# Two sets of exponentials: exponents first, copies moved to VectorE, one piece moved behind the set

## The chip, the cores and the metric

The kernel runs on one core of a Trainium2 chip. A core has TensorE (PE, matrix products into PSUM), VectorE (DVE), ScalarE (ACT, functions looked up in a table that has to be loaded for each set of functions), GpSimd (POOL) and SyncE (SP), which here only issues DMAs. Each engine works through its own list of instructions in order and waits at semaphores for the others. The metric is the device time of one execution in microseconds; the figure for a kernel is the median of its runs.

## The reference

The reference computes one block of a network on an input of 2048 tokens by 448 channels: a modulation from a small vector, a layer norm, a long convolution by a state-space kernel (S4D), then a second layer norm and a token-mixing MLP with 1792 hidden units. What matters here is the convolution kernel:

```python
A = -jnp.exp(log_A_real) + 1j * A_imag
C = (C_real + 1j * C_imag) * dt[:, None]
P = jnp.exp((A * dt[:, None])[:, :, None] * pos[None, None, :])
K = 2.0 * jnp.einsum("dn,dnl->dl", C, P).real
y = jnp.fft.irfft(Uf * Kf[None, :, :], L2)[:, :, :L]
```

For each of 448 channels, 256 complex exponentials are evaluated at 2048 positions and summed to K; K is then convolved with the input by Fourier transforms of length 4096.

## The kernel before, in words

A position is split in two, l = 64 i + j, so that the sum over the 256 modes becomes a small matrix product of two factors, `E` (64 columns) and `G` (32 columns). The channels go by in 56 steps, each of 16 channels and one half of the modes; `st_kgen(s)` makes step s's part of K out of `E` and `G` on TensorE (64 small products into the PSUM tile `kg`, line 717).

The factors are magnitudes times sines and cosines. Magnitudes need ScalarE's table of exponentials and sines another table, so the kernel works in batches of eight steps: `window(s)`, called for s = 0, 8, ..., 48, makes the exponentials of the eight steps s to s + 7 in one go. For each e from 0 to 7 it issues two exponentials (`st_exp`, line 650, tile `mag`), then on TensorE the exponents of the next step (`st_exponents`, line 644, by the helper of line 627, tiles `xe` and `xg`), or behind the last of them the phases of step s (`st_phase`). The PSUM tiles `xe` and `xg` have two buffers each. GpSimd follows with two multiplications per step (`st_mag2`, lines 666 and 671). Behind the set come the eight steps themselves: `st_step` has six ScalarE functions (two absolute values, lines 683 and 684, written to `ab` and `gs`, and four sines, lines 685 to 688), four multiplications on VectorE (lines 692 to 696) and two on GpSimd (690 and 691).

Other work is laid in between. `st_s1` makes the first stage of K's Fourier transform for a pair of finished groups (product `y`, line 755) and copies it out of PSUM to `yk` (line 761). In the steps above 32 the convolution itself goes on in pieces, `piece(go, inside)`: a forward product (`pc_s2`, tile `kx`, line 809), a multiplication by the input's transform on VectorE (`pc_mul`, tiles `z`, line 817), an inverse product (`pc_inv`, tile `vv`, line 832) and a copy out of PSUM (`pc_out`, tile `vt`, line 842) that is stored by DMA. A piece that starts also loads what the piece three later needs (`pc_load`: `u`, line 781, and the table `si`, line 787). The tiles `y`, `kx` and `vv` share three PSUM buffers (`ms`); `kg` has one.

The order on TensorE, ScalarE, VectorE and GpSimd is the order in which the program issues the instructions (a manual schedule). SyncE's DMAs are ordered by a planner. Copies and multiplications that follow a product are not issued at once but kept in two lists, `act` and `dve`, and issued at the next `flush`: in the set once per e, in a step `dve` in the middle of `st_step` (`between`) and `act` behind it. So a copy on ScalarE of step s comes behind the six functions of step s + 1. `warm(n)` issues n products of constants without use, to keep TensorE busy; steps 8 k and 8 k + 1 have ten each.

Before the change, the inverse of piece 2 (then 7) stood in step 38 (46), the copies of that step's `y` were ScalarE's behind step 39 (47), the set had the `kg` product of step 39 (47) at e = 0, an inverse at e = 2, the start of a new piece at e = 4 and `y` at e = 5.

Of the kernel before, what the change touches and what calls it, by code (L numbers as in the profile page):

```python
# [29 lines left out]
NHALF = 2 * NG  # L30
BATCH = 8
# [201 lines left out]
def tile_adaln_s4d_mixer(ctx, tc, i, out):  # L233
# [19 lines left out]
    with ExitStack() as es:  # L253
# [124 lines left out]
        def flush(todo):  # L378
            while todo:
                todo.pop(0)()  # L380
# [260 lines left out]
        def st_exponents(s):  # L641
            g, h = divmod(s, 2)
            phs[s] = [pph.tile([P, 512], F32, tag=nm, name=nm) for nm in ("xe", "xg")]
            halves(phs[s], lex[g % 4][:, h * P : (h + 1) * P], tab[:, 2], True, True)

        def st_exp(s):
            mags[s] = mp.tile([P, 2, 512], F32, tag="mag", name="mag")
            pm = phs.pop(s)
            for k in range(2):
                S.activation(mags[s][:, k], pm[k], AF.Exp)  # L650

        def st_phase(s):

            g, h = divmod(s, 2)
            lhs = lph[g % 3][:, h * P : (h + 1) * P]
            pm = [pph.tile([P, 512], F32, tag=nm, name=nm) for nm in ("xe", "xg")]
            halves(pm, lhs, tab[:, 1], True, False)
            halves(pm, mg[:, 0], ones, False, False)
            halves(pm, mg[:, 1], ones, False, False)
            halves(pm, lhs, tab[:, 0], False, True)  # L660
            phs[s] = pm
# [37 lines left out]

        kgs, kss, made_k = {}, {}, [0]  # L700

        fresh, ready = [], []

        def mellow():
            ready.extend(fresh)
            fresh.clear()

        def st_kgen(s):
            g, h = divmod(s, 2)
            kg = kg_tile(g)  # L710
            made_k[0] += 1
            E, Gt = eg.pop(s)
            for m in range(4):
                for c in range(2):
                    for q in range(4):
                        d = 8 * (q // 2) + 2 * m + q % 2
                        T.matmul(  # L717
                            kg[32 * q : 32 * q + 32, m],
                            Gt[:, c, d],
                            E[:, c, d],  # L720
                            start=h == 0 and c == 0 and m == 0,
                            stop=h == 1 and c == 1,
                            skip_group_check=True,
                        )
            if h == 1:
                p, o = divmod(g, 2)
                if o == 0:
                    kss[p] = wp.tile([P, 2, 4, NJ], F32, tag="ks", name="ks")

                def copy():  # L730
                    S.copy(kss[p][:, o], kgs.pop(g)[:, 0:4])
                    if o:
                        dve.append(skip)

                def skip():
                    k0 = kss[p][:, :, :, 0:1]
                    G.tensor_tensor(k0, k0, dsk[:, g - 1 : g + 1, :, None], ALU.add)
                    fresh.append(p)

                act.append(copy)  # L740

        def st_s1(busy):

            if not ready:
                return False
            p = ready.pop(0)
            c, gl = divmod(p, NG // 4)
            ks = kss.pop(p)
            y1 = [pms.tile([P, 32, 2, 4, 2], F32, tag="ms", name="y1") for _ in range(2)]
            for o in range(2):  # L750
                for m in range(4):
                    for cc in range(2):
                        for q in range(2):
                            r = slice(64 * q, 64 * q + 64)
                            T.matmul(
                                y1[q][64 * cc : 64 * cc + 64, :, o, m], ks[r, o, m], wc[r, cc, r], start=True, stop=True
                            )

            def out(q, copy):
                o = yks[c][:, :, 2 * gl * GD : 2 * (gl + 1) * GD].rearrange("p k (g q m) -> p k g q m", g=2, q=2)  # L760
                copy(o[:, :, :, q], y1[q].rearrange("p k g m b -> p k g (m b)"))  # L761

            for q in range(2):
                (dve if busy else act).append(partial(out, q, V.tensor_copy if busy else S.copy))
            return True


# [223 lines left out]
                if k is not None:  # L991
                    f(k)

        def piece(go, inside=False):

            if pieces[1] < pieces[0]:
                n = pieces[1]
                pc_inv(n)
                (dve if inside else act).append(partial(pc_out, n, V.tensor_copy if inside else S.copy))
                pieces[1] += 1  # L1000
            if go:
                n = pieces[0]
                if n + 3 < 2 * NP:
                    pc_load(n + 3)
                pc_s2(n)
                dve.append(partial(pc_mul, n))
                pieces[0] += 1

        def window(s):
            if s:  # L1010
                aside.append(True)
            angle()
            logs(s == 8)
            if s == 8:
                u_scale()
                u_table(0)
                u_table(1)

            if s == 0:
                st_exponents(s)  # L1020
            for e in range(BATCH):
                st_exp(s + e)

                if e + 1 < BATCH:
                    st_exponents(s + e + 1)
                else:
                    st_phase(s)
                mellow()
                flush(dve)
                flush(act)  # L1030
                if s == 8 and e == 0:
                    tt(mod[1], mod[1], mod[2], ALU.mult)
                if s < 32:
                    more(WPACE[s // 8][e])
                if s == 0 and e >= 4:
                    u_stats(e - 4)
                if s == 8 and e in (3, 4):
                    modulation(0, e - 3)
                if s == 8 and e == 5:

                    G.tensor_tensor(mod[0], mod[0], mod[2], ALU.mult)
                if s and e < (2 if s <= 32 else 1):
                    st_kgen(s - (2 if s <= 32 else 1) + e)
                elif e == 5:
                    if s == 8:
                        yks[0] = y0.tile([P, 32, DC], F32, tag="yk", name="yk0")
                    st_s1(s > 16)

                for k, e0 in ((4, 1), (5, 3), (3, 6)) if s == 16 else ():
                    if e in (e0, e0 + 1):  # L1050
                        modulation(k, e - e0)

                if s == 8:
                    warm(7)
                if s in (8, 16):
                    some(u_rows, rows, (2, 2, 2, 2, 2, 0, 1, 1)[e])
                elif s == 24 and e in (0, 2, 4, 6, 7):
                    some(u_cols, cols, 1)

                if s >= 40 and e == 2:  # L1060
                    piece(False, True)
                if s >= 40 and e == 4:
                    piece(pieces[0] < NP, True)
                if s == 0 and e > 1:
                    st_mag2(e - 2)
                elif s and (e < 2 or s >= 32):
                    st_mag2(s + e)
                if s == 0 and e == 3:
                    for r in range(4):
                        dsk_copy(r)  # L1070
            aside.clear()
            if s == 0:

                S.activation(one, one, AF.Sin)
# [6 lines left out]
        for s in range(tail):  # L1081
# [11 lines left out]
            if s in late:  # L1093
                late[s]()
            if s < NHALF and s % BATCH == 0:
                window(s)
                if s == 0:
                    gp_ = right("gp", 3)
            if s % BATCH == 4:
# [12 lines left out]
            if s >= NHALF:  # L1112
                flush(dve)
                mellow()
            else:
                if s < 32 and s % BATCH > 1:
                    st_kgen(s - 2)
                if s % BATCH < 2:
                    warm(10)
                if (s + 1) % BATCH:  # L1120
                    st_phase(s + 1)
                elif s + 1 < NHALF:
                    st_exponents(s + 1)
                if s == 7:
                    warm(10)

                if s > 32 and s % BATCH:
                    st_kgen(s - 1)
                st_step(s, between)
# [4 lines left out]

            if s in (1, 2):
                x_load(4 + 4 * s, 4, G)
            free = s > 7 and not st_s1(s % BATCH == BATCH - 1)
            if s + 2 < 32 and (s + 2) % BATCH > 1 and s + 2 > 5:
                st_mag2(s + 2)

# [16 lines left out]
            if s == 31:  # L1157
                flush(dve)
                flush(act)
            if s > 32:  # L1160
                piece(pieces[0] < NP and (s % 2 == 1 or s >= NHALF))
            if s == 34:

                for t in (ft, b1, b2):
# [302 lines left out]
```

## Time and profile before

| | us |
|---|---|
| runs of the kernel before | 693.27, 698.49, 696.14 |
| median | 696.14 |
| span of the profiled execution | 693.5 |
| busy: PE, DVE, ACT, POOL | 628.4, 438.7, 446.6, 269.7 |
| set of step 40: table load, first exponential, first function of step 40 | at 260.14, 261.43, 270.92 |
| set of step 48: the same | at 302.19, 303.49, 313.93 |

The page gives no time of the profiled execution beside its span. Times in rows are microseconds from the start of the span; the second number of a row of instructions is how long it took. Rows in order of time merge neighbours of one kind (`x64`: 64 instructions). A bracket at the end says how long the engine stood idle before the instruction, and which instruction ended that. PEld is the loading of weights beside the products. The granted clock is the share of full clock at which TensorE was allowed to run.

### The profile page before, as it was taken

To read this page: it belongs to the slowest core of one execution; us is meant where nothing else is said; L and a number is where in the kernel's file an instruction comes from. 1 tells how busy PE (TensorE), PEld (TensorE's weight loads), DVE (VectorE), ACT (ScalarE), POOL (GpSimd) and SP (SyncE) were. 2 spreads that over 40 slices of the span, in tenths; PEclk is the share of its full clock that TensorE was granted. 3 is DMA by queue.
4 is the path that set the end of the run, shared out by engine and by line. 5 is a ranking of instruction groups with operands and counts; after the bars stand their busy time and mean duration, and the time that the engine had idled before them with its cause. 6 is when DMAs were issued, how large, how long until landed. Compare 5 with 4: busy or idle time off the path is not lost.

```text
span 693.5 us, 19319 instructions
## 1 busy us (share of the span) xinstructions
PE 628.4 (91%) x7706; PEld 452.3 (65%) x7706; DVE 438.7 (63%) x835; ACT 446.6 (64%) x847; POOL 269.7 (39%) x349
## 2 busy tenths in 40 slices
PE   0878999999888889988898899999999999999997
PEld 0444555444345545555554567778899999999997
DVE  7886789789785574856745578876732364444441
ACT  5888598999689889989856768887322352222220
POOL 7694669588499667767635300000000000000000
PEclk9989999999999899999899999999999999999999
DMA  7595557598786354443479899955574445556540
GB/s 174 176 208 130 196 186 247 200 225 258 219 253 189 94 131 140 131 125 104 116 251 341 280 269 261 262 151 142 177 226 108 146 132 160 160 162 170 163 131 26
DMA packets 100322, 125.16 MB, mean 180 GB/s; under 512 B 13860, under 2 KB 81992, under 8 KB 100232
## 3 DMA queue, kind: packets, MB, share of 16 engines
q1 hardware_dynamic: 99288, 121.30, 61.0%
q0 software_dynamic: 944, 2.62, 1.6%
q8 instruction: 61, 1.00, 0.6%
q14 instruction: 29, 0.24, 0.1%
HBM read 88.53 MB, written 34.87 MB: 178 GB/s over the span
## 4 chain that ended last, share of the span: by engine, by line
PE 62%; ACT 12%; POOL 8%; DMA 6%; DVE 5%; issue 5%; SPq 1%; DVEq 0%; POOLq 0%; ACTq 0%
PE o L1434 7%; PE acc L1270 6%; PE o L1433 6%; PE o L1435 6%; PE acc L1271 6%; PE acc L1272 6%; PE xe L627 5%; PE kg L717 4%; POOL G L691 3%; POOL G L690 2%; PE xg L627 2%; PE vv L832 2%; PE kx L809 2%; PE kg L639 2%; PE y L1307 2%
## 5 line engine op out<-in xcount | busy, mean ns | idle before, releaser
L218 ACT CAST whi<-w 128x896 fp32r<-128x896 f32 x64 | 59.7, 938 | 134.3 <-PE o L1434 82.6
L227 DVE TENSOR_TENSOR wlo<-w,whi 128x896 fp32r<-128x896 f32 x64 | 68.1, 1085 | 40.6 <-ACT whi L218 40.6
L690 POOL TENSOR_TENSOR G<-mag,gs 128x512 f32<-128x512 f32 x56 | 71.8, 1282 | 46.0 <-ACT gs L686 45.9
L1270 PE MATMUL acc<-h3h,whi 128*128 128x448 f32 x224 | 82.9, 370 | 1.7 <-ACT h3h L1337 0.9
L1271 PE MATMUL acc<-h3l,whi 128*128 128x448 f32 x224 | 81.6, 364 | 0.2 <-DVE mean L1291 0.2
L1434 PE MATMUL o<-ul,whi 128*128 128x448 f32 x224 | 81.3, 363 | 0.0
L1433 PE MATMUL o<-uh,whi 128*128 128x448 f32 x224 | 81.2, 362 | 0.0
L1272 PE MATMUL acc<-h3h,wlo 128*128 128x448 f32 x224 | 80.7, 360 | 0.0
L1435 PE MATMUL o<-uh,wlo 128*128 128x448 f32 x224 | 80.6, 360 | 0.0
L717 PEld LDWEIGHTS kg<-E,G 128*32 128x32 f32 x3584 | 58.1, 117 | 31.7 <-issue 22.1
L717 PE MATMUL kg<-E,G 128*32 128x64 f32 x3584 | 68.2, 231 | 4.1 <-issue 4.1
L691 POOL TENSOR_TENSOR G<-mag,gs 128x512 f32<-128x512 f32 x56 | 71.8, 1281 | 0.0
L627 PE MATMUL xg<-tab,lph 64*128 64x512 f32 x112 | 62.9, 561 | 8.0 <-DVE E L696 3.5
L627 PE MATMUL xe<-tab,lph 64*128 64x512 f32 x112 | 63.6, 568 | 1.9 <-ACT gs L687 0.9
L1438 DVE TENSOR_TENSOR y<-o,x 128x448 f32<-128x448 f32 x16 | 10.0, 624 | 78.8 <-PE o L1435 78.8
L692 DVE TENSOR_TENSOR E<-m,xe 128x512 f32<-128x512 f32 x53 | 36.3, 684 | 35.2 <-ACT xe L685 25.1
L671 POOL TENSOR_TENSOR m<-mag,w 128x512 f32<-128x512 f32 x53 | 55.8, 1052 | 4.1
L1270 PEld LDWEIGHTS acc<-h3h,whi 128*128 128x128 f32 x224 | 42.0, 188 | 15.2 <-ACT h L1342 3.5
L817 DVE TENSOR_TENSOR z<-kx,u 128x448 f32<-128x448 f32 x48 | 28.4, 619 | 33.1 <-PE kx L809 30.5
L832 PE MATMUL vv<-z,si 64*64 64x224 f32 x512 | 36.8, 385 | 9.4 <-ACT yk L761 6.2
L627 PE MATMUL xe<-tab,lex 64*128 64x512 f32 x56 | 31.0, 569 | 15.7 <-POOL wm L874 14.8
L1433 PEld LDWEIGHTS o<-uh,whi 128*128 128x128 f32 x224 | 42.1, 188 | 3.4
(242 smaller groups left out, 1455.9 us busy)
## 6 DMA issues: line engine op xcount, KB each, us to landing
w<-in_B_w_dram SPq DMA_DIRECT2D x64, 224.0 KB
w<-in_B_w_dram SPq DMA_DIRECT2D x32, 448.0 KB
yu_d<-yt SPq DMA_DIRECT2D x16, 448.0 KB
yi<-yu_d SPq DMA_DIRECT2D x32, 224.0 KB
us_d<-uo SPq DMA_DIRECT2D x16, 448.0 KB
u<-us_d SPq DMA_DIRECT2D x64, 112.0 KB
v_d<-vt SPq DMA_DIRECT2D x32, 224.0 KB
vt<-v_d SPq DMA_DIRECT2D x14, 448.0 KB
```

Of the source, the lines that this page charges most:

```text
L218: self.nc.scalar.copy(hi, w)
L227: eng.tensor_tensor(lo, w, hi.bitcast(F32), ALU.subtract)
L627: T.matmul(out[k], lhs[r], rhs[r], start=start, stop=stop)
L690: G.tensor_tensor(Gt[:, 1], mg_, v32(sg), ALU.mult)
L691: G.tensor_tensor(Gt[:, 0], mg_, v32(cg_), ALU.mult)
L717: T.matmul(kg[32 * q : 32 * q + 32, m], Gt[:, c, d], E[:, c, d], start=h == 0 and c == 0 and m == 0, stop=h == 1 and c == 1, skip_group_ch ...
L1270: nc.tensor.matmul(acc[f], hi[:, fs], h3h[:, r], start=r == 0, stop=False)
L1271: nc.tensor.matmul(acc[f], hi[:, fs], h3l[:, r], start=False, stop=False)
L1272: nc.tensor.matmul(acc[f], lo[:, fs], h3h[:, r], start=False, stop=r == 15)
L1433: nc.tensor.matmul(o, hi[:, ks], uh[kh][:, k], start=kh == 0 and k == 0, stop=False)
L1434: nc.tensor.matmul(o, hi[:, ks], ul[kh][:, k], start=False, stop=False)
L1435: nc.tensor.matmul(o, lo[:, ks], uh[kh][:, k], start=False, stop=kh == 1 and k == 6)
```

## The change

It concerns the sets of steps 40 and 48 alone (the new function `late_window`, called in place of `window` for s > 32) and the steps around them:

- The copies of `y` of step 38 (46) go into a list `hold` and are issued on VectorE at the start of the set. In that step no piece is called: the inverse that stood there waits. Step 39 (47) starts its piece as before but runs no inverse (`back=False`).
- In the set the `kg` product of step 39 (47) stands at e = 1 behind the exponents, with its copy on VectorE; the two inverses that are left over stand at e = 3 and e = 5, `y` at e = 6. All copies there are VectorE's.
- No new piece starts in the set. It starts in step 40 (48) instead, with its loads; its inverse comes in step 41 (49), which also starts the next piece.
- The ten products of `warm` are left out in steps 40 and 48.

```diff
-        def st_kgen(s):
+        def st_kgen(s, to=act):
...
-                    S.copy(kss[p][:, o], kgs.pop(g)[:, 0:4])
+                    (V.tensor_copy if to is dve else S.copy)(kss[p][:, o], kgs.pop(g)[:, 0:4])
...
-                act.append(copy)
+                to.append(copy)
...
-        def st_s1(busy):
+        def st_s1(*to):
...
-                (dve if busy else act).append(partial(out, q, V.tensor_copy if busy else S.copy))
+                to[-q].append(partial(out, q, S.copy if to[-q] is act else V.tensor_copy))
...
-        def piece(go, inside=False):
+        def piece(go, inside=False, back=True):
 
-            if pieces[1] < pieces[0]:
+            if back and pieces[1] < pieces[0]:
...
+        def late_window(s):
+
+            flush(hold)
+            for e in range(BATCH):
+                st_exp(s + e)
+                if e + 1 < BATCH:
+                    st_exponents(s + e + 1)
+                else:
+                    st_phase(s)
+                mellow()
+                flush(dve)
+                flush(act)
+                if e == 1:
+                    st_kgen(s - 1, dve)
+                elif e in (3, 5):
+                    piece(False, True)
+                elif e == 6:
+                    st_s1(dve)
+                st_mag2(s + e)
...
-                if s >= 40 and e == 2:
-                    piece(False, True)
-                if s >= 40 and e == 4:
-                    piece(pieces[0] < NP, True)
...
-                window(s)
+                (late_window if s > 32 else window)(s)
...
-                if s % BATCH < 2:
+                if s % BATCH < 2 and s != 40 and s != 48:
                     warm(10)
...
-            free = s > 7 and not st_s1(s % BATCH == BATCH - 1)
+            held = s > 32 and s % BATCH == BATCH - 2 and s + 2 < NHALF
+            free = s > 7 and not st_s1(hold if held else dve if s % BATCH == BATCH - 1 else act)
...
-            if s > 32:
-                piece(pieces[0] < NP and (s % 2 == 1 or s >= NHALF))
+            if s > 32 and not held:
+                ends = s % BATCH == BATCH - 1 and s + 1 < NHALF
+                piece(pieces[0] < NP and (s % 2 == 1 or s >= NHALF or s in (40, 48)), back=not ends)
```

More of the change, by code (lines that the diff above doesn't have):

```diff
@@ L700, in tile_adaln_s4d_mixer @@
         kgs, kss, made_k = {}, {}, [0]
-        fresh, ready = [], []
+        fresh, ready, hold = [], [], []
         def mellow():
@@ L1046, in window @@
                         yks[0] = y0.tile([P, 32, DC], F32, tag="yk", name="yk0")
-                    st_s1(s > 16)
+                    st_s1(dve if s > 16 else act)
                 for k, e0 in ((4, 1), (5, 3), (3, 6)) if s == 16 else ():
```

## The prediction

> **What bounds the kernel now.** I read the page first, then the chain of waits from 245 to 450 us, then the instructions in order of time around the sets of exponentials of steps 40 and 48 and the steps behind them, then TensorE's busy time with its granted clock by short stretches.
>
> ```profile
> PE 62%; ACT 12%; POOL 8%; DMA 6%; DVE 5%; issue 5%; SPq 1%; DVEq 0%; POOLq 0%; ACTq 0%
> ```
>
> ```profile
> 256.53 0.62 ACT xg L688
> 257.16 0.52 ACT yk L761
> 257.72 1.76 PE vv L832 x14
> ```
>
> The chain runs through PE for 62% of the span, but most of that is the MLP at the end. At the two sets it changes hands: ScalarE's sines of step 39, its copies of `yk`, then PE's piece, and from there PE's own products to the end of the set. The order of instructions at the entries to the sets of 40 and 48 says why:
>
> ```profile
> 257.05 1.10 ACT L761 COPY yk<-y 128x512 f32<-128x512 f32 x2
> 259.53 0.59 ACT L842 COPY vt<-vv 128x224 f32<-128x224 f32 x2 [1.38 <-PE vv L832]
> 260.14 1.28 ACT L650 ACT_TABLE_LOAD   x1
> 261.43 0.60 ACT L650 ACTIVATE mag<-xe 128x512 f32<-128x512 f32 x1
> ...
> 270.92 0.60 ACT L683 ACTIVATE ab<-xe 128x512 f32<-128x512 f32 x1
> ```
>
> ```profile
> 299.37 0.62 ACT L688 ACTIVATE xg<-ab 128x512 f32<-128x512 f32 x1
> ...
> 303.49 0.60 ACT L650 ACTIVATE mag<-xe 128x512 f32<-128x512 f32 x1
> 303.98 0.59 ACT L650 ACTIVATE mag<-xg 128x512 f32<-128x512 f32 x1
> ...
> 313.93 0.60 ACT L683 ACTIVATE ab<-xe 128x512 f32<-128x512 f32 x1
> ```
>
> The last sine ends at 256.53 + 0.62 = 257.15. Two copies of `yk` follow; the inverse products of a piece wait for their PSUM; ScalarE then idles 1.38 for that piece and copies it; only then come the table load and the first exponential. The sets run from first exponential to first `ab` in 270.92 - 261.43 = 9.49 and 313.93 - 303.49 = 10.44. Sixteen exponentials at a pitch of 303.98 - 303.49 = 0.49 are 7.8, so inside the sets TensorE is what ends last:
>
> ```profile
> 262.41 0.50 PE L627 MATMUL xe<-tab,lex 64*128 64x512 f32 x1
> 262.84 1.10 PE L717 MATMUL kg<-E,G 128*32 128x64 f32 x64
> ...
> 264.53 0.99 PE L832 MATMUL vv<-z,si 64*64 64x224 f32 x16
> ...
> 268.27 1.16 PE L755 MATMUL y<-wc,ks 64*64 64x64 f32 x64
> ...
> 270.19 0.58 PE L627 MATMUL xe<-tab,lph 64*128 64x512 f32 x1
> ```
>
> A block starts 0.07 before the one ahead of it ends (262.84 against 262.41 + 0.50), so from start to next start I count exponents 0.43, `kg` 1.03, a piece's inverse 0.92, `y` 1.09.
>
> **Entry.** The change takes the `yk` copies and the piece's copy off ScalarE here, and the inverse off PE. ScalarE then loads its table right behind the last sine, and 260.14 to 261.43 puts the first exponential 1.29 later: 257.15 + 1.29 = 258.44 instead of 261.43, and 299.37 + 0.62 + 1.29 = 301.28 instead of 303.49. That is 3.0 and 2.2 us earlier. The exponents it needs stand on PE behind the `y` of step 38, with no copy ahead of them now (by the chain it was `yk` that the piece between them waited for), so they are there before the last sine ends.
>
> **Inside the set.** PE's list has as many blocks as before: a second inverse comes in, the forward product (`kx`) goes out. Counted from the first exponential: its two reads end at 0.49 + 0.59 = 1.08, so the exponents for the third one end at about 1.65 and `kg` starts at 1.6. Then `kg` 1.03, two exponents 0.9, inverse 0.92, exponents 0.43 lead to 4.9; the next exponents wait for the buffer of the fifth exponential until 5.3; exponents 0.43, inverse 0.92, exponents 0.5 lead to 7.1; `y` waits 0.1 for VectorE's copy of the second inverse and takes 1.09, to 8.3. The phase product takes 1.2 by a later row (279.85 to the start of `kg` at 281.07, quoted below), and `ab` follows its end by 0.15 (270.19 + 0.58 to 270.92): 9.7. Against 9.49 and 10.44 that is 0.2 longer and 0.7 shorter. The sets together: -3.0 + 0.2 - 2.2 - 0.7 = -5.7. Bounds: no shorter than 13 x 0.49 + 0.59 + 1.2 + 0.15 = 8.3, when the phase product follows the seventh exponential at once (-8.5 in all), no longer than the 10.44 seen (-4.3).
>
> **What else is added there, and what hides it.** VectorE gets the held `yk` copies, the copy of `kg`, and one more piece:
>
> ```profile
> 262.53 1.16 DVE L817 TENSOR_TENSOR z<-kx,u 128x448 f32<-128x448 f32 x2 [4.06 <-PE kx L809]
> 265.57 0.69 DVE L842 COPY vt<-vv 128x224 f32<-128x224 f32 x2 [1.89 <-PE vv L832]
> ...
> 269.49 1.29 DVE L761 COPY yk<-y 128x512 f32<-128x512 f32 x2 [0.36 <-PE y L755]
> ```
>
> The `yk` pair is 1.29, the piece 0.69. A `kg` copy on VectorE does not occur in this trace: between 0.35 (half the 0.69) and 0.65 (half the 1.29), I take 0.38, nearest to ScalarE's 0.37 for it. That is 1.29 + 0.69 + 0.38 = 2.4 us into idle stretches of 4.06 and 1.89; without that cover `y` would start later by as much. Behind the held copies queues the multiplication `z`, whose reader, the inverse, now comes 3 us later. GpSimd's work in the set is unchanged and hangs on the exponentials alone: it is done 1.38 before its first `G` is wanted, in a set of 9.49, and in one of 9.7 that idle time doesn't shrink.
>
> ```profile
> 274.48 1.28 POOL L690 TENSOR_TENSOR G<-mag,gs 128x512 f32<-128x512 f32 x1 [1.38 <-ACT gs L686]
> ```
>
> The moved piece's loads move with it; the `u` load of piece 7 waits until piece 4 is multiplied, now in step 41, and holds SP's queue with a store of `v_d` and the next `lph` and `lex` loads behind it. Piece 7 is multiplied in step 46 and the loads behind serve steps 46 and later, so I cost this at nothing; without that cover the price would be one `u` load on the path.
>
> **The step behind.** Piece 4 now starts in step 40, is multiplied in step 41, and its inverse and piece 5's forward product both stand at the end of step 41.
>
> ```profile
> 277.72 0.68 DVE L693 SCALAR_TENSOR_TENSOR E<-mag,xe 128x512 f32<-128x512 f32 x1
> ...
> 281.83 1.15 DVE L817 TENSOR_TENSOR z<-kx,u 128x448 f32<-128x448 f32 x2
> ```
>
> ```profile
> 277.91 1.10 PE L717 MATMUL kg<-E,G 128*32 128x64 f32 x64
> 278.94 0.98 PE L809 MATMUL kx<-yk,si 128*64 128x224 f32 x8
> 279.85 0.50 PE L627 MATMUL xe<-tab,lph 64*128 64x512 f32 x1
> 281.07 1.10 PE L717 MATMUL kg<-E,G 128*32 128x64 f32 x64
> 282.60 1.05 PE L832 MATMUL vv<-z,si 64*64 64x224 f32 x16 [0.42 <-DVE z L817]
> ```
>
> ```profile
> 282.24 0.37 ACT L731 COPY ks<-kg 128x256 f32<-128x256 f32 x1 [0.19 <-PE kg L717]
> ```
>
> In these rows' times: `z` of piece 4 comes behind L693, 278.40 + 1.15 = 279.5; an inverse ends 0.67 after its `z` (283.65 against 282.98), 280.2; then `kx` 0.91, 281.1; the phase product 1.22, 282.3; `kg` 1.10, 283.4. ScalarE's copy of that `kg` then starts at 283.45 instead of 282.24, and behind it stand all sines of step 43: 1.2 us lost per set. The piece's own copy only moves from step 41's end to step 42's. Bounds 0 (ScalarE catches up from its small idle times) and 2.0 (the idle of step 34 below). Twice 1.2 gives +2.4.
>
> **The ten warming products taken out of steps 40 and 48.**
>
> ```profile
> 273.94 1.27 PE L639 MATMUL kg<-ones 128*128 128x256 bf16 x10
> 275.39 0.47 PE L627 MATMUL xe<-tab,lph 64*128 64x512 f32 x1 [0.19 <-issue]
> 276.83 0.47 PE L627 MATMUL xg<-tab,lph 64*128 64x512 f32 x1 [0.97 <-DVE E L696]
> ```
>
> ```profile
> 230.17:233.59 3.42, 1.50 (x9) 1.00 0.22 60
> 233.59:237.00 3.41, 3.41 (x73) 0.50 0.20 60
> ...
> 274.55:277.96 3.41, 2.25 (x19) 1.00 0.42 126
> ```
>
> ```profile
> 233.64 1.93 PE L717 MATMUL kg<-E,G 128*32 128x64 f32 x64
> 235.51 1.69 PE L809 MATMUL kx<-yk,si 128*64 128x224 f32 x8
> 239.40 0.37 ACT L731 COPY ks<-kg 128x256 f32<-128x256 f32 x1 [2.01 <-PE kg L717]
> ```
>
> The columns of the middle fence are the stretch, its length, PE's busy time, the granted clock and the DMA. A stretch of 3.4 us with 1.50 busy is followed by 3.41 us at clock 0.50; one with 2.25 busy, step 41 as it is now, is not (the `kx` of 278.94 behind it takes 0.98). Without the first ten products the idle time ahead of step 41's phase product grows from 0.19 by 1.27, less an overlap of 0.1, to about 1.35 (the inverse that leaves step 40 and the `kx` that comes last the same), and 0.97 follows it, with 0.47 of products between. A stretch that holds both waits has 1.1 busy. I put the threshold at 1.8, between 1.50 and 2.25. If the stretches lie at random against the kernel, it is undercut where at most 0.7 of the idle time falls outside: 0.6 + 0.7 + 0.7 = 2.0 of 3.41 positions, 60% per set, so one of the two sets is the likeliest count. The price: `kg` 1.93 for 1.10 and `kx` 1.69 for 0.98, 1.5 together, of which 0.4 lies under the wait for `z`: +1.1. Bounds 0 and 2.0, ScalarE's idle time in the last row, at the end of such a stretch.
>
> **Sum.** -5.7 + 2.4 + 1.1 = -2.2. The profiled span is 693.5; the runs have the median 696.1 (693.3 to 698.5), and nothing in the trace says which part of that 2.6 is outside the span, so I take the difference over: 696.1 - 2.2 = 693.9.
>
> **Rivals.** *Clock stays up.* If the threshold lies lower than I read it, only the 1.2 per set comes back: -3.3, 692.8. The Trainium skill, "TensorE: Matmul & The Clock Gate", section "Why this matters for your kernels", asks only that no idle gap exceed about 3 us; by that rule no clock would drop and the sum would be -3.3. The trace speaks against it: from 230.17 to 233.59 PE is busy 1.50 in nine products, so its gaps sum to 1.92, and the half clock follows.
> *Nothing comes back.* The step behind has room after all: -5.7, 690.4. For it: the 0.42 for which the inverse of step 42 waits for `z` shows some slack on PE. Against: ScalarE already waits 0.19 for that `kg`, so any lateness of it is passed on.
> *Slower.* The half clock holds the step behind in both sets for two stretches, not one: 2 x 3.41 / 2 = 3.4 us of products lost beside the 1.2, 4.6 against the 2.85 that a set gains: +1.75 each, +3.5, 699.6. It decides once the clock costs a set more than 1.65. For it: the 2.01 that ScalarE lost to one such stretch; against: PE's list behind the gap is dense, which should end the half clock after one.
> *No effect.* The table load might stay late for a reason not seen here, so that the entry gains nothing: between 0 and +2.4, about 697.
>
> **Chances.** Forecast 0.50, clock stays up 0.15, nothing comes back 0.20, slower 0.10, no effect 0.05. About 1%, 7 us, is what a measurement tells from no change: 689.1 and 703.1. No case reaches these alone; with the runs' scatter of some 2.6 to either side and the 8.3 bound of the set, faster gets 0.09, slower 0.04, the rest 0.87. The range 689.5 to 698.0 goes down to *nothing comes back*, less 1 for the scatter, and up past *no effect*; *slower* is left out.
>
> **What would show it.** Right: the table load directly behind the last sine, no ScalarE idle ahead of it, first exponential to `ab` near 9.7, no half clock ahead of `kg` at the entries; in step 42 ScalarE idle over 1 us ahead of its `kg` copy; a half clock behind one of the sets. Wrong: a wait for the exponents at the entry; `y` held by VectorE's copies; step 43's `ab` no later against step 40's; or SP holding a load that a product waits for.

## The result, and the profile after

The changed kernel takes 692.0 us, the kernel before 696.1 (medians of 20 runs each): ratio 0.9936, 95% interval 0.9913 to 0.9958, 4.1 us faster. The profiled execution has a span of 690.4 us and took 692.2; it was 693.5 before. The forecast was 693.9, 2.2 faster.

ScalarE at the two entries, in order of time (start, duration, line; in brackets the idle time ahead and what ended it):

```profile
253.98 0.62 ACT L688 ACTIVATE xg<-ab 128x512 f32<-128x512 f32 x1
254.62 1.28 ACT L650 ACT_TABLE_LOAD   x1
255.92 0.60 ACT L650 ACTIVATE mag<-xe 128x512 f32<-128x512 f32 x1
...
265.44 0.60 ACT L683 ACTIVATE ab<-xe 128x512 f32<-128x512 f32 x1 [1.25 <-PE xg L627]
...
297.61 0.62 ACT L688 ACTIVATE xg<-ab 128x512 f32<-128x512 f32 x1
...
299.55 0.60 ACT L650 ACTIVATE mag<-xe 128x512 f32<-128x512 f32 x1
...
309.05 0.60 ACT L683 ACTIVATE ab<-xe 128x512 f32<-128x512 f32 x1 [1.25 <-PE xg L627]
```

The table load stands right behind the last sine, and the first exponential follows that sine's end by 1.32 us (255.92 against 254.60), where it was 4.28 and 3.50. From first exponential to first `ab` both sets take 9.5 (265.44 - 255.92, 309.05 - 299.55). VectorE's new work in the first set:

```profile
255.84 1.28 DVE L761 COPY yk<-y 128x512 f32<-128x512 f32 x2
...
258.65 0.42 DVE L731 COPY ks<-kg 128x256 f32<-128x256 f32 x1 [0.47 <-PE kg L717]
...
262.63 0.69 DVE L842 COPY vt<-vv 128x224 f32<-128x224 f32 x2 [1.46 <-PE vv L832]
```

It idles ahead of each copy but the held ones, and the profile shows no wait of TensorE or ScalarE for one of these copies. Behind the set it looks otherwise. TensorE in steps 41 and 42, then ScalarE's copies of `kg` in steps 42 and 50:

```profile
269.89 0.47 PE L627 MATMUL xe<-tab,lph 64*128 64x512 f32 x1 [1.53 <-ACT gs L687]
271.35 0.76 PE L627 MATMUL xg<-tab,lph 64*128 64x512 f32 x1 [0.99 <-DVE E L696]
...
273.35 1.93 PE L717 MATMUL kg<-E,G 128*32 128x64 f32 x64
275.21 1.77 PE L832 MATMUL vv<-z,si 64*64 64x224 f32 x16
276.91 1.32 PE L809 MATMUL kx<-yk,si 128*64 128x224 f32 x8
```

```profile
280.44 0.37 ACT L731 COPY ks<-kg 128x256 f32<-128x256 f32 x1 [2.81 <-PE kg L717]
...
322.73 0.37 ACT L731 COPY ks<-kg 128x256 f32<-128x256 f32 x1 [2.43 <-PE kg L717]
```

ScalarE now idles 2.81 and 2.43 ahead of that copy; it was 0.19. TensorE's busy time and granted clock by stretches of 3.41 us (stretch, its length, busy time with the number of products, granted clock, the DMA engines' busy share and GB/s) show a half clock, 0.50, at these places:

```profile
267.38:270.80 3.42, 1.45 (x10) 1.00 0.20 63
270.80:274.21 3.41, 2.86 (x41) 0.50 0.09 29
274.21:277.62 3.41, 3.41 (x61) 0.50 0.50 137
...
311.77:315.19 3.42, 0.89 (x5) 1.00 0.05 18
315.19:318.60 3.41, 3.41 (x71) 0.50 0.01 1
```

A stretch with 1.45 busy, then two at half clock behind the first set (the first of them is not full either, 2.86 busy); one with 0.89 busy, then one behind the second. Before, the half clock fell on the entries instead, as these stretches of the kernel before show:

```profile
254.07:257.48 3.41, 1.34 (x54) 1.00 0.58 159
257.48:260.89 3.41, 3.17 (x45) 0.50 0.16 28
...
298.44:301.85 3.41, 1.29 (x16) 1.00 0.54 152
301.85:305.26 3.41, 3.41 (x74) 0.50 0.48 144
```

So in this profile the half clock was moved, not removed. For the comparisons below I cut each set into three parts, all read off ScalarE's instructions: from the end of the last sine of step 39 (47) to the first exponential, from there to the sines' table load (1.1 behind the first `ab`), and from there to the start of the `kg` copy of step 42 (50). What lies between the two sets, from that copy to the last sine of step 47, is 17.73 to 17.79 in every kernel that keeps this copy on ScalarE.

| kernel | first set | second set | half-clock stretches in them |
|---|---|---|---|
| before, first profile | 4.28 + 10.60 + 10.21 = 25.1 | 3.50 + 11.55 + 10.22 = 25.3 | entry; entry |
| before, second profile | 4.18 + 10.83 + 10.22 = 25.2 | 3.50 + 11.56 + 10.22 = 25.3 | entry; entry |
| changed, first | 1.32 + 10.62 + 13.90 = 25.8 | 1.32 + 10.60 + 12.58 = 24.5 | two behind; one behind |
| changed, second | 1.32 + 10.62 + 12.54 = 24.5 | 1.31 + 10.61 + 13.90 = 25.8 | one behind; two behind |
| changed, third | 1.32 + 12.03 + 11.21 = 24.6 | 1.31 + 10.62 + 11.21 = 23.1 | one at the entry; none |

### The profile page after: what moved, and what is told of

The parts are those of the page before. It is cut to its first block, busy times and chain, and to the rows that moved or that the text cites. A ratio compares the mean times of both kernels' runs of the same rounds, so it can differ in the third digit from the quotient of the medians.

```text
span 690.4 us, 19264 instructions
## 1 busy us (share of the span) xinstructions
PE 622.6 (90%) x7686; PEld 448.9 (65%) x7686; DVE 443.5 (64%) x845; ACT 443.0 (64%) x837; POOL 269.3 (39%) x349
## 4 chain that ended last, share of the span: by engine, by line
PE 61%; ACT 11%; DMA 8%; POOL 6%; DVE 6%; issue 5%; SPq 2%; POOLq 0%; ACTq 0%; DVEq 0%
PE o L1451 7%; PE o L1453 7%; PE o L1452 6%; PE acc L1288 6%; PE acc L1289 6%; PE acc L1290 6%; PE xe L627 5%; PE kg L717 5%; PE xg L627 3%; DMA w<-in_B_w_dram 3%; PE vv L832 2%; POOL G L690 2%; DMA u<-us_d 2%; POOL G L691 2%; PE kx L809 2%
## 5 line engine op out<-in xcount | busy, mean ns | idle before, releaser
L683 ACT ACTIVATE ab<-xe 128x512 f32<-128x512 f32 x56 | 33.9, 604 | 18.0 <-PE xg L627 13.1
L1289 PEld LDWEIGHTS acc<-h3l,whi 128*128 128x128 f32 x224 | 42.0, 187 | 3.9 <-DVE h3l L1362 0.9
L1453 PEld LDWEIGHTS o<-uh,wlo 128*128 128x128 f32 x224 | 42.0, 188 | 3.3
```

Of the source, the lines that this page charges most:

```text
L1289: nc.tensor.matmul(acc[f], hi[:, fs], h3l[:, r], start=False, stop=False)
L1453: nc.tensor.matmul(o, lo[:, ks], uh[kh][:, k], start=False, stop=kh == 1 and k == 6)
```

## The experiments

The theory I set out with: the sets gain what the forecast says; the second piece in step 41 gives 1.0 to 1.2 us per set back at full clock, and each half-clock stretch behind a set another 1.1 to 1.6. The main rivals: the wait comes from the order of the pieces alone and the clock lies beside it; or the whole gain is the half clock that left the entry.

### The changed kernel again

> The changed kernel once more, beside the variants on one chip. Both theories: about 4.1 us under the kernel before (ratio 0.994). The theory says that the sets gain some 5.5 us and that the steps behind them give part of it back; in the profile ScalarE waits over 1 us ahead of its copy of kg in steps 42 and 50, and more where a half clock fell on step 41 or 49.

Ratio 0.9959 (0.9924 to 0.9993), median 692.1 against 695.6. Both sets again have half-clock stretches behind them, one and two (table).

### The warming products put back

```diff
-                if s % BATCH < 2 and s != 40 and s != 48:
+                if s % BATCH < 2:
```

> The changed kernel with the ten warming products of steps 40 and 48 put back. Theory (half clock behind the sets costs 1.1 to 1.6 us each, on top of 1.2 us from the second piece): no half clock in steps 41 and 49, ScalarE's wait ahead of the kg copy in steps 42 and 50 falls from 2.8 and 2.4 to about 1.2, time 2 us under the changed kernel, about 6 under the kernel before. Rival (the wait comes from the order of the pieces alone, the clock lies beside it): waits as in the changed kernel, time within 0.5 us of it.

Ratio 0.9929 (0.9891 to 0.9967), median 690.1: 2 us under the changed kernel run beside it. The two ratios' intervals overlap, so the runs alone don't show these 2 us; the profile shows where they can come from. TensorE and ScalarE at the same place:

```profile
267.44 1.26 PE L639 MATMUL kg<-ones 128*128 128x256 bf16 x10
268.85 0.47 PE L627 MATMUL xe<-tab,lph 64*128 64x512 f32 x1
270.30 0.47 PE L627 MATMUL xg<-tab,lph 64*128 64x512 f32 x1 [0.99 <-DVE E L696]
...
275.53 1.10 PE L717 MATMUL kg<-E,G 128*32 128x64 f32 x64
```

```profile
275.04 0.61 ACT L842 COPY vt<-vv 128x224 f32<-128x224 f32 x2
276.70 0.37 ACT L731 COPY ks<-kg 128x256 f32<-128x256 f32 x1 [1.05 <-PE kg L717]
```

The wait of 1.53 is gone, no half clock falls behind either set, `kg` takes 1.10 and ScalarE waits 1.05 and 1.06. The sets are 1.31 + 10.62 + 11.20 = 23.1, both. So at full clock the second piece costs 11.20 - 10.21 = 1.0; a stretch at half clock adds 12.55 - 11.20 = 1.35, a second one the same again. That the clock lies beside the wait is out.

### The warming products alone taken out of the kernel before

```diff
-                if s % BATCH < 2:
+                if s % BATCH < 2 and s != 40 and s != 48:
```

> The kernel before with only this edit: the ten warming products of steps 40 and 48 left out. Theory: TensorE's busy time in the stretch of step 41 falls to about 1.1 of 3.41 us and in some 60% of cases a half clock follows; 1 to 2 us slower than the kernel before in all. Rival (one inverse less in step 41 leaves room that hides a half clock): within 0.5 us of the kernel before although the granted clock falls.

Ratio 1.0020 (0.9988 to 1.0051), median 695.1 against 695.6. In us the interval runs from 0.8 faster to 3.6 slower, so the 1 to 2 expected is neither shown nor excluded. The profile has the stretch: behind both sets the third part is 11.65 and 11.76 for 10.21, and ScalarE waits 1.64 and 1.75 ahead of the copy that waited 0.19:

```profile
278.96 0.37 ACT L731 COPY ks<-kg 128x256 f32<-128x256 f32 x1 [1.64 <-PE kg L717]
```

In this profile the first entry happened to keep its clock (3.49 + 10.00), so the first set's sum, 25.1, doesn't show its stretch; the second set's is 26.8.

### The new piece kept in the set

```diff
-                    piece(False, True)
+                    piece(e == 5 and pieces[0] < NP, True)
...
-                piece(pieces[0] < NP and (s % 2 == 1 or s >= NHALF or s in (40, 48)), back=not ends)
+                piece(pieces[0] < NP and (s % 2 == 1 or s >= NHALF), back=not ends)
```

> The changed kernel with the new piece started in the set at e = 5 and not in step 40 (48), so that steps 40 and 41 have one inverse and one start between them as in the kernel before. Theory: the set grows by one forward product, 9.5 to 10.4 us, and ScalarE's wait ahead of the kg copy of step 42 (50) loses its 1.2 us, so that only what a half clock leaves stays; together 0 to 1.5 us under the changed kernel. Rival (the second piece isn't what delays step 42): the wait stays over 2 us and the kernel is 1.8 us slower than the changed one.

Ratio 0.9893 (0.9838 to 0.9948), median 688.1 of 8 runs between 684.1 and 695.9: faster than expected by the medians, with the widest scatter of all; the profile is of the slowest of the eight. The set grew by 0.8 (11.39 and 11.41), as expected; the third part has half-clock stretches in both sets (13.07, 11.62), so this profile can't separate the two causes. The kernel that has both edits, further down, does.

### The kg copy of steps 42 and 50 on VectorE, with the warming products

```diff
-                    st_kgen(s - 1)
+                    st_kgen(s - 1, dve if s in (42, 50) else act)
```

> The warming products put back, and in steps 42 and 50 the copy of kg on VectorE and not on ScalarE, so that step 43's sines don't stand behind it. Theory (ScalarE's wait for that kg is what the second piece costs): from the sines' table load of step 40 to step 43's first function the 1.0 us that is lost at full clock comes back in each set; 2 us under the variant with the warming products alone. Rival (step 43 waits for PE in another way, by its phases or by the piece's own copy): within 0.5 us of it.

Ratio 0.9927 (0.9899 to 0.9956), median 690.0, against 690.1 without it: the rival. ScalarE's functions of steps 43 and 44:

```profile
278.34 0.61 ACT L842 COPY vt<-vv 128x224 f32<-128x224 f32 x2
279.01 0.60 ACT L683 ACTIVATE ab<-xe 128x512 f32<-128x512 f32 x1
...
282.01 0.60 ACT L842 COPY vt<-vv 128x224 f32<-128x224 f32 x2
282.73 0.60 ACT L683 ACTIVATE ab<-xe 128x512 f32<-128x512 f32 x1
...
287.00 0.37 ACT L731 COPY ks<-kg 128x256 f32<-128x256 f32 x1 [1.17 <-PE kg L717]
```

Step 43 starts as early as hoped, but step 44 then comes 3.72 behind it instead of 3.46, and ahead of step 45 ScalarE waits 1.17 for the next `kg`, where it waits 0.20 with the copy left on ScalarE. From the last sine of step 39 to that of step 47 only 0.3 of the 1.0 is left (40.6 for 40.9). So the copy's place was not what cost the 1.0: TensorE is late, and ScalarE meets that at the next `kg` instead.

### The held copies on ScalarE

```diff
-                to[-q].append(partial(out, q, S.copy if to[-q] is act else V.tensor_copy))
+                to[-q].append(partial(out, q, V.tensor_copy if to[-q] is dve else S.copy))
```

> The changed kernel with the held copies of y on ScalarE, ahead of the table load at the start of the set, the order of all else kept. Theory (at the entry ScalarE's own list decides): the first exponential comes 1.1 us later behind the last sine, 2.4 for 1.3 us, the set keeps its 10.6 us to the sines' table load, 2.2 us slower than the changed kernel in all. Rival (inside the set TensorE decides and its exponents are there early): the set gets shorter by what the entry loses, no change.

Ratio 1.0014 (0.9985 to 1.0042), median 694.6: in the runs the gain is gone.

```profile
255.47 0.62 ACT L688 ACTIVATE xg<-ab 128x512 f32<-128x512 f32 x1
255.99 1.10 ACT L761 COPY yk<-y 128x512 f32<-128x512 f32 x2
257.11 1.28 ACT L650 ACT_TABLE_LOAD   x1
```

The entry takes 2.32 and 2.31, 1.0 more each, and the set keeps 10.61 and 10.62 to the sines' table load. TensorE's early exponents buy nothing back: the set follows its first exponential. The two entries are 2.0 us of what the runs lose. The sums, 24.1 and 25.5 (a half-clock stretch behind the second set), are still 0.8 us together under those of the kernel before, where the runs show nothing left.

### The new piece kept in the set, with the warming products

> The new piece started in the set at e = 5, and the warming products of steps 40 and 48 put back. Theory: entry 1.3, the set 11.4 us to the sines' table load, from there 10.2 us to the kg copy of step 42 as in the kernel before, no half clock: 22.9 us against 23.1 with the warming products alone, so 0.4 us less in all, and 5 to 6 us under the kernel before. Rival (the second piece, not the clock, costs more than 1.0): 2 us or more under the variant with the warming products alone.

This kernel has the edits of both sections, the warming products put back and the piece kept in the set. Ratio 0.9923 (0.9892 to 0.9955), median 689.0, the smallest scatter (687.6 to 690.8). ScalarE from the end of the first set to the `kg` copy of step 42:

```profile
266.06 0.60 ACT L683 ACTIVATE ab<-xe 128x512 f32<-128x512 f32 x1 [1.12 <-PE xg L627]
267.16 1.28 ACT L685 ACT_TABLE_LOAD   x1
...
277.38 0.37 ACT L731 COPY ks<-kg 128x256 f32<-128x256 f32 x1 [0.20 <-PE kg L717]
```

Both sets take 22.9: 1.32 + 11.38 + 10.22 and 1.31 + 11.40 + 10.21. With the piece in the set the wait in step 42 is back to 0.20, so the 1.0 is the second piece's; the set pays 0.8 for it. This kernel is faster than the kernel before, and its median is 3 us under the changed kernel's (689.0 against 692.0), though the two ratios' intervals overlap.

### Warming products at the entry of the kernel before

```diff
+            if s in (38, 46):
+                warm(14)
             if s > 32:
                 piece(pieces[0] < NP and (s % 2 == 1 or s >= NHALF))
```

> The kernel before with only this edit: fourteen warming products ahead of the inverse in steps 38 and 46, where TensorE waits for PSUM, so that no half clock falls on the entry. Theory (a half clock at the entry costs the kernel before 1.4 us a set, the order of the copies 0.6 more): 23.7 us from the last sine to the kg copy of step 42 where it was 25.1 and 25.3; up to 2.8 us under the kernel before. Rival (the change's whole gain is the half clock that it takes from the entry): as fast as the changed kernel, 4 us under the kernel before.

Ratio 0.9966 (0.9938 to 0.9993), median 691.4 against 695.0. ScalarE at the first entry:

```profile
257.38 0.62 ACT L688 ACTIVATE xg<-ab 128x512 f32<-128x512 f32 x1
257.90 1.10 ACT L761 COPY yk<-y 128x512 f32<-128x512 f32 x2
259.60 0.59 ACT L842 COPY vt<-vv 128x224 f32<-128x224 f32 x2 [0.59 <-PE vv L832]
260.21 1.28 ACT L650 ACT_TABLE_LOAD   x1
```

The copies stand ahead of the table load as before, but the sets take 3.50 + 9.99 + 10.22 = 23.7 and 3.63 + 9.98 + 10.21 = 23.8: 1.45 per set less, without a copy moved. By the theory 2.8 us, by the ratio 0.5 to 4.3; the rival's 4 lies inside that too, and by its median this kernel is as fast as the changed one. The sets speak for the theory: at full clock on both sides they still differ by 0.6. The profile is of the slowest of the twelve runs (697.9), but what made it slow lies outside the sets: in no other profile does the rest of the kernel take as long.

### Both kernels once more

> The kernel before, profiled again at another position against the clock's stretches. What is open: the two sets of its first profile (25.1 and 25.3 us from the last sine to the kg copy of step 42 and 50) and those of the changed kernel (25.8 and 24.5) differ by nothing, and the runs by 4 us. If the first profile is typical, its sets take 25.1 to 25.3 again, with a half clock at both entries, and the difference must lie in the same instructions ahead of step 39 and behind step 55 (607.6 us together, 604.5 in the changed kernel). If the first profile was lucky, the sets take 26 us or more.

> The changed kernel, profiled a third time. If a half clock behind the sets is typical, both sets again have one or two stretches behind them (24.5 or 25.8 us); if the two profiles so far were unlucky, one of the sets shows 23.1 us, as with the warming products put back, and ScalarE's wait ahead of the kg copy of step 42 is 1.05 us there.

Ratios 1.0013 (0.9981 to 1.0045) for the kernel before against itself and 0.9946 (0.9916 to 0.9976) for the changed one. The kernel before repeats its sets within 0.2 us, with half clock at both entries again; that an entry can also keep its clock was seen once, with the warming products taken out. The changed kernel shows what a change of luck does: in the first set the half clock falls on the entry, in the second on nothing, and ScalarE's wait is 1.05 there in both. TensorE at that first entry, then ScalarE:

```profile
252.93 0.45 PE L755 MATMUL y<-wc,ks 64*64 64x64 f32 x12 [1.49 <-issue]
...
253.74 1.93 PE L717 MATMUL kg<-E,G 128*32 128x64 f32 x64
255.60 1.74 PE L809 MATMUL kx<-yk,si 128*64 128x224 f32 x8
```

```profile
278.46 0.37 ACT L731 COPY ks<-kg 128x256 f32<-128x256 f32 x1 [1.05 <-PE kg L717]
```

## Why the prediction was right, and where it was not

**Entry.** Right: the copies and the piece ahead of the table load were ScalarE's whole delay. 1.32 from last sine to first exponential where 1.29 was said, -3.0 and -2.2 us as said, though 0.8 of the 3.0 was half clock (with products in the gap the entry takes 3.50). The held copies on ScalarE give back 1.0 per set. The sign *no half clock ahead of `kg` at the entries* held in five sets of six; in the third profile one fell there.

**Inside the set.** Nearly right: 9.5 for 9.7, and TensorE's phases are what ends last (the 1.25 ahead of `ab`). VectorE's copies cost nothing, and its `kg` copy takes 0.42, inside the bounds of 0.35 and 0.65.

**The step behind.** Right in place and close in size: ScalarE waits for `kg` in step 42, 1.0 at full clock where 1.2 was said; keeping the piece in the set takes the wait back to 0.20. *Nothing comes back* is out.

**Half clock.** Right that the missing warming products bring it: of the twelve profiled sets of kernels with these products none has half clock behind it, of the twelve without nine have. The threshold of 1.8 us busy held for 1.45 and 0.89, but it is not sharp (last section). Mis-sized twice: the price of a stretch is 1.35, not 1.1, and in six profiled sets of the changed kernel four have it behind them and two of those have two, where I counted one in two sets. Against a second stretch I held that TensorE's list behind the gap is dense; where the second came, the first had 2.86 and 2.90 busy, where it didn't, 3.41. *Slower*, with two stretches behind both sets, is what happened behind one set of each of the first two profiles. *Clock stays up* is out. The rule of the Trainium skill, "TensorE: Matmul & The Clock Gate", section "Why this matters for your kernels", to leave no idle gap of over some 3 us, was not enough here: the longest gaps behind the first set were 1.53 and 0.99 us, and the clock fell.

**The sum.** The direction is right and the time lies in the range, but the account behind it is not the one I gave, and that the forecast came so near is in part luck. The -5.7 were booked on the order of the copies; in the first profiles entry and set gain 6.1. Warming products alone take 1.45 per set off the kernel before, so 2.9 of that were the half clock at the two entries. At full clock on both sides the change's order is worth 23.8 - 23.1, some 0.6 per set: 2.2 gained at the entry (3.5 to 1.3), 0.6 lost in the set (10.0 to 10.6) and 1.0 behind it. The table's sums average 25.2 before and 24.7 after, so in the profiles the sets yield about 1.0 us together, not 2.2.

The runs say 4.1 (3.6 between the means of all 42 runs of the changed kernel and of the 90 of the one before whose clock is on record, a run of 1139 us left out). In the profiles most of the difference lies in instructions that both kernels share: up to the last sine of step 39 and from that of step 55 on, the two profiles of the kernel before have 607.6 and 608.2 us, the three of the changed kernel 604.5, 604.9 and 603.7. But this part scatters as much among variants that leave it alone. The kernel before has 603.4 there with the warming products of steps 40 and 48 taken out and 613 with those at the entry put in; the changed kernel's variants have 605.4 to 608.5. So the profiles can't say that the change made it shorter. The clock is not enough either: the 42 and the 90 runs spend on average 30.0 and 32.1 us at half clock (worked out as in the last section), and within the two groups a us at half clock goes with 0.30 and 0.42 us of time, so the 2.0 us between them are worth less than 1. Some 1.5 to 2.5 us of the 3.6 stay without a cause. No run was made that holds the clock fixed.

## What to carry to other kernels

A transfer of work off the engine that gates a stage pays what its own list says, here to 0.1 us at the entry. But where a second engine has a clock that follows its load, every idle time that an order opens or closes is also a matter of clock: ask where the gap goes, and fill it with cheap products before counting the gain. By its sets (22.9 us each) the version to take is the one with the piece kept in the set and the warming products left in; from the other two that put these products back the runs don't tell it apart.

## What the hardware showed that was not expected

The granted clock goes with much of the scatter. For the 20 runs of the changed kernel, the time at half clock, worked out as twice the missing share of the granted clock times the span, lies between 14 and 40 us, and correlates with the run's time at 0.76: 0.34 us of time for each us at half clock. So single runs, or medians of a few, can differ by half a per cent by luck with the stretches, and a single profile shows one position against them only: of the changed kernel's three, no two have the same stretches in the sets.

How much TensorE has to do for the clock to stay is nearly, but not quite, a matter of its busy time in the stretch. In the third profile of the changed kernel the products ahead of the first entry paused once, for 1.49 us inside `y`, which left 1.92 busy in the stretch from 250.37; half clock followed, and `kg` took 1.93. Behind the two sets of the same profile stretches with 1.88 and 1.87 busy were not followed by it. With all twelve profiles cut from 60 us on into stretches of 3.41 us, half clock followed 55 of the 56 full-clock stretches with under 1.7 us busy, 8 of the 24 with 1.7 to 1.95, 11 of the 449 from there to 3.2, and none of the 1578 above. The ends of products are modelled, so what decides in the middle band is not shown.
